# Moving the first pair's token tiles into memory that attention frees first, and loading them at attention's end

## The chip, the cores and the metric

The kernel runs on one core of a Trainium2 chip. The metric is the time of one execution on the device in microseconds (us), taken as the median over several runs. Five engines work side by side, each through its own queue in order: TensorE (PE; its weight loads are shown apart as PEld), VectorE (DVE), ScalarE (ACT), GpSimd (POOL) and SyncE (SP, which here only issues DMA transfers). A DMA that must wait for something holds up whatever stands behind it on the engine that issues it.

## The reference

An attention with mixing of heads before and after the softmax, and a feed-forward part on its result. Cut to what is computed:

```python
# q, k, v: (8, 12, 448, 64); w_pre, w_post: (12, 12)
scores = 1 / sqrt(64) * q @ k^T
scores = einsum('bhij,hg->bgij', scores, w_pre)
attn = exp(scores - max(scores))
attn = attn / (sum(attn) + 1e-9)
attn = einsum('bhij,hg->bgij', attn, w_post)
x = (attn @ v).transpose(0, 2, 1, 3).reshape(3584, 768)
h = x @ w_in            # w_in: (768, 2048)
g = h - tanh(h)
out = g @ w_out         # w_out: (2048, 768)
```

## The kernel before

**Numbers in two parts.** A product of 32-bit numbers is made of three matmuls on rounded parts: each operand is split into a high part (a rounding copy on ScalarE) and a low part (the operand minus its high part, on VectorE); `products` adds high x high, high x low and low x high in one PSUM bank. Names ending in `h` and `l` are such parts. A low part is written over the tile that held the operand.

**Attention** runs as a list of places, `for p in range(NPL + 3)`. At each place it mixes, exponentiates and normalizes one pair of row groups and does jobs planned beforehand (scores, transposes, values). Its results go to DRAM (`xs`, one tensor for each of the 8 batches), through the tile `x` and the DMA queue kept by hand in `dma`, `issue` and `now`. Beside it, until place NPL-3, runs the conversion of the feed-forward weights into parts and sums (`conv`), which go to DRAM too (`wis`, `sss`, `wos`, `tss`).

**The feed-forward part** takes the 3584 tokens in 7 blocks of 512. Block 0 is computed plainly: `Block0.step` runs for f = 0 to 17, where step f loads the weights of f+2 (`load_w0`, three buffers, so the load of f+2 waits until TensorE is through with f-1), calls `between(f)`, multiplies (18 matmuls into one of two PSUM banks `ps_h`), and copies the bank out (L347). Every two steps one gate, h - tanh(h), is computed for two tiles by class `Gate`: `a1` and `a2` on ScalarE (four passes), `d1` and `d2` on VectorE (three), then `a3` on ScalarE (a Relu that serves as a mask), `d3` and `d4` on VectorE (a product and a predicated copy). For small h a rational formula is used, for others tanh; the mask decides. The first two steps of block 0 and its gates run while attention's last values are computed.

The other 6 blocks go in 3 pairs (`pair_step`, 8 steps for each pair), in a scheme with seven products in place of eight. Its right operands are token tiles: `b11`, `b21`, `b22` and `t1` to `t4`, each with parts `h` and `l`, 14 tiles of 3x512 numbers per partition. Four of them (`b11l`, `b21l`, `t3l`, `b22l`) are loaded by `load_xq`, six DMAs each, and `xq_jobs` then makes the 14 tiles from them in eleven jobs: differences on VectorE, high parts on ScalarE (L569), low parts on VectorE (L572). `WA` is the order in which the seven products read them: b11, b21, t2, t1, t3, b22, t4. The products of a step share two banks X and Y of `ps_h`; products 2, 4 and 6 add onto X, which must have been copied out to `h01` or `h23` before. The second gate of a step (`Late`) is computed during the next step; its results and sums of them (`ga`, `gb`, `gs`) are stored by POOL. Between products stand units of the output product (`res.units`), which reads stored gates (`gl<-go`, `gl<-gs`) and weights (`w<-wo`, `w<-ts`). After each pair some units are held back, and the jobs of the next pair's token tiles are run between them.

**Memory.** SBUF is used as two stacks of tile pools, "left" and "right". A pool that is opened over memory of a closed one makes the first user of each tile wait for the last user of what lay there. During attention the left stack holds `ld` (k and q tiles and their parts), `sp` (scores) and `cv` (conversion); it is closed at place NPL-3 and `open_early` opens the first feed-forward pools there. The right stack holds attention's constants, `kp` (`x`, `at`, `vr`) and `gp` (`t`, `e`, `wr`), which are used until attention's end; `open_late` opens pools there after it. In the kernel before, the working tiles of the gates (pool `rw`), the tiles `gl` and `gh` and two weight tiles lie on the left, and all token tiles but one (pool `xqb`) on the right. `close_plain`, at step f=15, closes the pools of block 0's weights and tokens and opens those of the pair's weights (`wa`) there.

**Order.** `in_order`, at the end, fixes the order of every engine's instructions as the program wrote them. So the place in the program where a job stands is its place in the engine's queue.

Of the kernel before, what the change touches and what calls it, by code (L numbers as in the profile page):

```python
# [150 lines left out]
def kernel_body(  # L151
# [71 lines left out]
    def pool(name, bufs, side, stack=ctx):  # L223
        return stack.enter_context(tc.tile_pool(name=name, bufs=bufs, side=side, reuse_waits="tile"))

    def open_early():
        ff.rw = pool("rw", 1, "left")
        ff.bias = pool("bias", 1, "left").tile([P, 2 * LINE], F32, name="bias", tag="bias")
        nc.gpsimd.memset(ff.bias[:, 0:1], GATE_A[1])
        nc.gpsimd.memset(ff.bias[:, 1:2], GATE_B[1])  # L230
        nc.gpsimd.memset(ff.bias[:, 2:3], -0.25)
        ff.gpl, ff.gph, ff.xr = pool("gpl", 3, "left"), pool("gph", 2, "left"), pool("xr", 1, "left")
        ff.w2a, ff.xqa = pool("w2a", 1, "left"), pool("xqa", 1, "left")
        ff.plain = ctx.enter_context(ExitStack())
        ff.w0, ff.xp = pool("w0", 3, "left", ff.plain), pool("xp", NK, "left", ff.plain)

# [7 lines left out]

    def open_late():
        rest_of_line(ctx)
        ff.xqb, ff.ca = pool("xqb", 1, "right"), pool("ca", 3, "right")
        ff.ps_y = ctx.enter_context(tc.tile_pool(name="ps_y", bufs=1, space=PSUM, side="left"))

    def close_plain():  # L250
        ff.plain.close()
        ff.w2b, ff.wap, ff.cb = pool("w2b", 1, "left"), pool("wa", 7, "left"), pool("cb", 9, "left")

    def work(tag, n=2):
        return ff.rw.tile([P, n, TB], F32, name=tag, tag=tag)


    def runs(b):
# [34 lines left out]

    class Gate:

        def __init__(self, h):
            self.h = h

        def a1(self):
            self.u, self.qa = work("u"), work("qa")  # L300
# [13 lines left out]
            nc.vector.scalar_tensor_tensor(out=self.qa, in0=self.qb, scalar=GATE_B[2], in1=self.qa, op0=ALU.add, op1=ALU.mult)  # L314

        def a3(self):
            nc.scalar.activation(self.qb, self.u, AF.Relu, bias=ff.bias[:, 2:3], scale=1.0)

        def d3(self, out):
            nc.vector.tensor_mul(out, self.qa, self.u)  # L320

        def d4(self, out):
            nc.vector.copy_predicated(out, self.qb.bitcast(I32), self.t)


    class Block0:
# [36 lines left out]
    class Results:  # L363
# [38 lines left out]
        def more_w2(self, upto):  # L402
            while self.n_w2 < min(upto + 1, len(self.w2s)):
                x = self.n_w2 % 3
                if self.deep_w2 is not None:
                    x = (self.n_w2 - self.deep_w2) % (len(XQ) + 3) - len(XQ)
                if x < 0:
                    w = ff.xqb.tile([P, HK, TB], F32R, name=XQ[x] + "h", tag=XQ[x] + "h")
                    w = w.rearrange("p c t -> p (c t)").rearrange("p (c t n) -> p c t n", t=2, n=P)
                else:  # L410
                    w = (ff.w2a if x < 2 else ff.w2b).tile([P, NK, 2, P], F32R, name=f"w2{x}", tag=f"w2{x}")
                ff.w2[self.n_w2] = w
                self.w2s[self.n_w2][1](w)
                self.n_w2 += 1

        def more_gr(self, upto):
            while self.n_gr < min(upto + 1, len(self.grs)):
                x = -1
                if self.deep_gr is not None:
                    x = (len(XQ) - 1 - self.n_gr + self.deep_gr) % (len(XQ) + 2) - 3  # L420
                if x < 0:
                    g = ff.gpl.tile([P, 2, TB], F32R, name="gl", tag="gl")
                else:
                    g = ff.xqb.tile([P, HK, TB], F32R, name=XQ[x] + "l", tag=XQ[x] + "l")[:, :2]
                ff.gr[self.n_gr] = g
                self.grs[self.n_gr](raw(g))
                self.n_gr += 1
# [46 lines left out]
        def c_tile(self):  # L474
            x = self.n_c % 12
            self.n_c += 1
            return (ff.ca if x < 3 else ff.cb).tile([P, HK, P], F32, name="c", tag="c")

        def y_tile(self, x):
            return ff.ps_y.tile([TT, TB], F32, name=f"y{x}", tag=f"y{x}")  # L480
# [68 lines left out]

    def x_tiles(*names):  # L550
        for x in names:
            p = ff.xqa if x == "t4l" else ff.xqb
            ff.xs[x] = p.tile([P, HK, TB], F32R, name=x, tag=x)

    def load_xq(name, b, h):
        x_tiles(name)
# [5 lines left out]
    def xq_jobs():  # L562

        def sub(x, y):
            nc.vector.tensor_sub(xr, x if x is xr else raw(ff.xs[x]), y if y is xr else raw(ff.xs[y]))

        def high(x, src):
            x_tiles(x + "h")
            nc.scalar.copy(ff.xs[x + "h"], src)  # L569

        def low(x, src):
            nc.vector.tensor_sub(ff.xs[x + "l"], src, raw(ff.xs[x + "h"]))  # L572

        def both(x):
            high(x, raw(ff.xs[x + "l"]))
            low(x, raw(ff.xs[x + "l"]))

        xr = ff.xr.tile([P, HK, TB], F32, name="xr", tag="xr")
        sub("t3l", "b11l")
        yield  # L580
        both("b11")
        yield
        x_tiles("t1l")
        high("t1", xr)
        low("t1", xr)
        yield
        sub("b22l", xr)
        yield
        x_tiles("t2l")
        high("t2", xr)  # L590
        low("t2", xr)
        yield
        sub("b21l", xr)
        yield
        x_tiles("t4l")
        high("t4", xr)
        low("t4", xr)
        yield
        both("b21")
        yield  # L600
        sub("b22l", "t3l")
        yield
        high("t3", xr)
        low("t3", xr)
# [56 lines left out]
    def pair_step(s, q, late, units, between):  # L661
# [62 lines left out]
    with ExitStack() as st:  # L724
# [508 lines left out]
        for p in range(NPL + 3):  # L1233
# [48 lines left out]
    xq = iter(())  # L1282

    def xq_loads(s):
        ba, bb = 2 * s + 1, 2 * s + 2
        for x, b, h in (("b11l", ba, 0), ("b21l", ba, 1), ("t3l", bb, 0), ("b22l", bb, 1)):
            yield from load_xq(x, b, h)

    xq, xl = xq_jobs(), xq_loads(0)
    res = Results()  # L1290
    ff.n_wa, ff.stored = 0, [0] * NS

    def between0(f):
        if f >= 3:
            for _ in range(4 if f % 2 else 2):
                next(xl, None)
        if f in (10, 12):
            res.more_w2((f - 10) // 2)
        if f in (13, 15):
            res.more_gr((f - 13) // 2)  # L1300
# [13 lines left out]
    for s in range(NS):  # L1314
# [15 lines left out]
        else:  # L1330
            res.deepen()
        job = partial(next, xq, None)
        jobs = [
            [late.v0], [late.v1, late.v2], [late.v3], [late.v4], [late.v5, job], [job, job], [job, job], [job, job],
            [job, job], [job, job],
        ]
        n = HELD[s] + AHEAD[s]
        for i in range(0, n, 2):
# [43 lines left out]
```

## Time and profile before

| | us |
|---|---|
| median of 3 runs (least to greatest) | 1756.36 (1755.81 to 1759.52) |
| profiled execution | 1768.5 |
| its span, first to last instruction | 1766.8 |
| TensorE busy | 1692.2 |
| VectorE busy | 1232.0 |
| ScalarE busy | 1145.3 |
| first matmul of block 0, f=0 (L285) | 868.09 |
| first matmul of the first pair | 945.38 |

The times of the profile are us from the start of the span. A row of the order of time gives start, length, engine, line of the kernel, operation, what is written from what is read, shapes, how many in a row, and in square brackets how long the engine stood idle before it and what released it. A row of waits gives who waited for whom, total us, how often, the longest. A row of groups gives busy us, mean ns of one, then the idle time before. A row of windows gives the busy time of each engine in a stretch, the clock granted to TensorE (1.00 is full), the busy share of the DMA engines and what they moved in GB/s.

### The profile page before, as it was taken

Reading aid. Unit: us, or ns where it says so; the run is one execution under the profiler, and the core shown is the slowest. Engines: PE = TensorE matmul, PEld = TensorE weight load, DVE = VectorE, ACT = ScalarE, POOL = GpSimd, SP = SyncE. Lnnn points to the kernel's source line nnn. Section 1 sums busy time; section 2 is a strip of 40 time slices with the busy share of each in tenths; the row PEclk is TensorE's granted clock in tenths of the full one; section 3 lists DMA queues with packets and bytes.
Section 4 is the critical chain, followed back from the end, with each engine's and each line's share of the span. In section 5 each row is a group of like instructions: output and inputs, shape, how many; then the busy total and the mean of one; then the engine's idle time right before and its main releaser. Section 6 shows DMA issues by size and latency. Waiting matters only on the chain.

```text
span 1766.8 us, 41167 instructions
## 1 busy us (share of the span) xinstructions
PE 1692.2 (96%) x16068; PEld 1399.9 (79%) x16068; DVE 1232.0 (70%) x2119; ACT 1145.3 (65%) x2016; POOL 489.1 (28%) x702
## 2 busy tenths in 40 slices
PE   8999999999999999999997999899999799999999
PEld 6777777777777677777775788788888788989999
DVE  5676777766777767775368899668777767778432
ACT  5776777768878777876476677455666456666331
POOL 1355455555555545451100011011001101001000
PEclk9998999999999989999998999999999999999999
DMA  8778789788887978865497789989889879888994
GB/s 184 201 226 238 226 253 273 223 256 236 246 259 233 263 227 246 258 203 173 166 309 269 243 305 310 318 279 328 324 303 366 320 251 334 300 313 319 405 415 156
DMA packets 322289, 475.09 MB, mean 269 GB/s; under 512 B 105264, under 2 KB 255280, under 8 KB 322096
## 3 DMA queue, kind: packets, MB, share of 16 engines
q1 hardware_dynamic: 305660, 414.34, 73.0%
q0 software_dynamic: 16128, 57.68, 8.3%
q8 instruction: 128, 2.10, 0.5%
q14 instruction: 65, 0.53, 0.1%
q10 hardware_dynamic: 308, 0.43, 0.1%
HBM read 274.73 MB, written 120.59 MB: 224 GB/s over the span
## 4 chain that ended last, share of the span: by engine, by line
PE 77%; DMA 6%; ACT 6%; DVE 6%; issue 3%; SPq 1%; POOL 1%; DVEq 0%; ACTq 0%; POOLq 0%
PE ps_o L945 14%; PE ps_m L987 8%; PE ps_p L906 8%; PE ps_h L285 7%; PE ps_h L286 6%; PE ps_h L288 6%; PE ps_q L862 6%; PE y L527 6%; PE y L525 6%; PE y L526 6%; DMA vr<-in_v_dram 1%; PE ps_m L828 1%; DMA t3l<-xs 1%; ACT e L917 1%; ACT at L955 1%
## 5 line engine op out<-in xcount | busy, mean ns | idle before, releaser
L945 PEld LDWEIGHTS ps_o<-wr,e 60*112 60x112 f32 (+1 forms) x5760 | 308.0, 176 | 46.6 <-POOL wr L928 12.4
L945 PE MATMUL ps_o<-wr,e 60*112 60x60 f32 (+1 forms) x5760 | 317.7, 260 | 17.6 <-ACT at L955 12.3
L915 DVE TENSOR_REDUCE mx<-ps_p 128x1 f32<-128x448 f32 x360 | 207.2, 617 | 165.0 <-PE ps_p L906 164.8
L917 ACT ACTIVATE e<-ps_p,mx 128x448 f32<-128x448 f32 x360 | 225.7, 634 | 106.6 <-DVE mx L915 98.7
L955 ACT COPY at<-ps_o 112x960 f32<-112x960 f32 x156 | 153.7, 985 | 88.3 <-PE ps_o L945 87.6
L928 POOL TENSOR_TENSOR wr<-wpost,zs 128x120 f32<-128x120 f32 x180 | 69.8, 388 | 437.6 <-DVE zs L927 330.1
L906 PE MATMUL ps_p<-t,wpre 60*64 60x448 f32 (+1 forms) x1440 | 186.1, 585 | 4.7 <-DMA t<-s 3.5
L987 PEld LDWEIGHTS ps_m<-at,vr 112*64 112x64 f32 x3072 | 152.2, 140 | 29.2 <-ACT at L962 11.2
L987 PE MATMUL ps_m<-at,vr 112*64 112x120 f32 (+1 forms) x3072 | 166.7, 266 | 5.4 <-ACT at L962 3.1
L525 PE MATMUL y<-w,gh 128*128 128x384 f32 x448 | 153.7, 343 | 5.5 <-DMA w<-ts 3.7
L527 PE MATMUL y<-w,gl 128*128 128x384 f32 x424 | 145.7, 344 | 8.5 <-DVE gl L443 8.4
L526 PE MATMUL y<-w,gh 128*128 128x384 f32 x448 | 152.8, 341 | 0.0
L862 PEld LDWEIGHTS ps_q<-kk,qh 64*120 64x120 f32 (+1 forms) x768 | 62.0, 182 | 88.9 <-issue 61.8
L862 PE MATMUL ps_q<-kk,qh 64*120 64x448 f32 (+1 forms) x768 | 127.3, 408 | 2.2 <-DVE kk L814 1.4
L867 DVE COPY s<-ps_q 120x448 f32<-120x448 f32 (+1 forms) x192 | 112.9, 615 | 11.3 <-PE ps_q L862 11.1
L301 ACT ACTIVATE u<-h 128x1024 f32<-128x1024 f32 x56 | 59.5, 1062 | 67.4 <-DVE h L704 66.5
L867 ACT COPY s<-ps_q 120x448 f32<-120x448 f32 (+1 forms) x192 | 95.5, 539 | 7.0 <-PE ps_q L862 6.7
L657 POOL DMA_DIRECT2D gs<-gb x24 | 17.2, 718 | 297.7 <-DVE gb L656 282.1
L525 PEld LDWEIGHTS y<-w,gh 128*128 128x128 f32 x448 | 86.0, 192 | 11.2 <-ACT u L301 4.0
L437 ACT CAST gh<-gl 128x1024 fp32r<-128x1024 f32 x61 | 63.5, 1040 | 47.6 <-DMA gl<-gs 21.3
L527 PEld LDWEIGHTS y<-w,gl 128*128 128x128 f32 x424 | 81.4, 192 | 10.3 <-DVE gl L443 10.1
L526 PEld LDWEIGHTS y<-w,gh 128*128 128x128 f32 x448 | 85.9, 192 | 3.4
(370 smaller groups left out, 3895.5 us busy)
## 6 DMA issues: line engine op xcount, KB each, us to landing
t<-s SPq DMA_DIRECT2D x342, 210.0 KB
wa<-ss SPq DMA_DIRECT2D x96, 384.0 KB
w<-wo SPq DMA_DIRECT2D x43, 768.0 KB
gl<-gs SPq DMA_DIRECT2D x62, 512.0 KB
wa<-wi SPq DMA_DIRECT2D x72, 384.0 KB
w<-ts SPq DMA_DIRECT2D x35, 768.0 KB
gs<-gs POOLq DMA_DIRECT2D x24, 768.0 KB, 8.9
cr<-in_moe_w_in_dram SPq DMA_DIRECT2D x48, 256.0 KB
```

Source lines behind the costliest of these rows:

```text
L285: nc.tensor.matmul(ph, w[:, c, 0], xh, start=start and c == 0, stop=False, skip_group_check=True)
L525: nc.tensor.matmul(y, gh[:, tok], wh, start=first, stop=False, skip_group_check=True)
L526: nc.tensor.matmul(y, gh[:, tok], wl, start=False, stop=False, skip_group_check=True)
L527: nc.tensor.matmul(y, gl[:, tok], wh, start=False, stop=last, skip_group_check=True)
L862: nc.tensor.matmul(ps[:n, :S], qx[a, hp, :], kx[a, hp % 2], start=(x == 0), stop=(x == 2))
L867: eng(sts[i][:n, 2 * hp + j, :], ps[:n, :S])
L906: nc.tensor.matmul(pss[r][halves[j], :], wpre[k, :], ts[j][k, :], start=True, stop=True)
L915: nc.vector.tensor_reduce(out=mx, in_=ps, axis=AX.X, op=ALU.max, negate=True)
L917: nc.scalar.activation(e, ps, AF.Exp, bias=mx, scale=1.0, accum_out=zs[:, 0, r : r + 1])
L945: nc.tensor.matmul(ps[:CP, j, c * GP : (c + 1) * GP].rearrange("p (h i) -> p h i", i=GI)[:, :, r * GH : (r + 1) * GH], e[k, c * CP : (c + ...
L955: nc.scalar.copy(ats[i0][:, :, :, at : at + 2 * GI].rearrange("p c h (j i) -> p j (c h) i", j=2), ps[:CP, :, : NC * GP].rearrange("p j (x ...
L987: nc.tensor.matmul(pv[j * D : (j + 1) * D, r, :n], vt[:, j, c, :], ats[i][:, c, 2 * hp + j, :n], start=(c == 0), stop=(c == NC - 1),)
```

## The change

Pools are moved: the left stack, from place NPL-3 on, holds the tiles `h01` and `h23` of the gates (pool `hid`), the difference tile `xr` and eleven of the fourteen token tiles (`xqa`). The other gate tiles, `gl`, `gh` and two weight tiles go to the right stack, opened at attention's end, with the three token tiles named in `LATER`. Of the twelve tiles `c` one instead of three lies on the right.

The loads of the first pair's four tiles move from steps f=3 to 8 of block 0 into attention's last places, NPL-2 to NPL+2 (2, 3, 3, 2 and 2 pieces of two DMAs), in the order b11l, t3l, b22l, b21l. The first job on them is issued before step f=1, the others by a list of steps up to f=14. Before, the jobs stood at f=6, 8 and 10 to 15 with three more in the pair's first step. The order of the eleven jobs is changed for all pairs. After the first and second pairs, nine instead of eleven jobs are run among the held units, and two in the next pair's first step.

Step f=2 of block 0, the first with a gate, now stands after `now()` and `open_late()`, not before.

The mask of block 0's gates and of the second gate of each pair step goes to a tile of its own, the one of `gs`, instead of over `qb`; the first gate of a pair step keeps `qb`.

```diff
     def open_early():
-        ff.rw = pool("rw", 1, "left")
+        ff.hid = pool("hid", 1, "left")
...
-        ff.gpl, ff.gph, ff.xr = pool("gpl", 3, "left"), pool("gph", 2, "left"), pool("xr", 1, "left")
-        ff.w2a, ff.xqa = pool("w2a", 1, "left"), pool("xqa", 1, "left")
+        ff.xr, ff.xqa = pool("xr", 1, "left"), pool("xqa", 1, "left")
...
     def open_late():
         rest_of_line(ctx)
-        ff.xqb, ff.ca = pool("xqb", 1, "right"), pool("ca", 3, "right")
+        ff.rw, ff.gpl, ff.gph = pool("rw", 1, "right"), pool("gpl", 3, "right"), pool("gph", 2, "right")
+        ff.w2a, ff.xqb, ff.ca = pool("w2a", 1, "right"), pool("xqb", 1, "right"), pool("ca", 1, "right")
...
-        ff.w2b, ff.wap, ff.cb = pool("w2b", 1, "left"), pool("wa", 7, "left"), pool("cb", 9, "left")
+        ff.w2b, ff.wap, ff.cb = pool("w2b", 1, "left"), pool("wa", 7, "left"), pool("cb", 11, "left")

     def work(tag, n=2):
-        return ff.rw.tile([P, n, TB], F32, name=tag, tag=tag)
+        return (ff.hid if tag in ("h01", "h23") else ff.rw).tile([P, n, TB], F32, name=tag, tag=tag)
+
+    LATER = ("b21h", "b22h", "t4h")
+
+    def x_tile_of(x):
+        return (ff.xqb if x in LATER else ff.xqa).tile([P, HK, TB], F32R, name=x, tag=x)
...
         def a3(self):
-            nc.scalar.activation(self.qb, self.u, AF.Relu, bias=ff.bias[:, 2:3], scale=1.0)
+            self.mk = work("gs", 3)[:, :2] if self.own_mask else self.qb
+            nc.scalar.activation(self.mk, self.u, AF.Relu, bias=ff.bias[:, 2:3], scale=1.0)
...
         def d4(self, out):
-            nc.vector.copy_predicated(out, self.qb.bitcast(I32), self.t)
+            nc.vector.copy_predicated(out, self.mk.bitcast(I32), self.t)
...
         sub("t3l", "b11l")
         yield
+        x_tiles("t1l")
+        parts("t1")
+        yield
+        sub("b22l", "t3l")
+        yield
+        parts("t3")
+        yield
+        nc.vector.tensor_add(xr, xr, raw(ff.xs["b11l"]))
+        yield
         both("b11")
         yield
         x_tiles("t2l")
-        high("t2", xr)
-        low("t2", xr)
+        parts("t2")
         yield
         sub("b21l", xr)
         yield
...
         both("b21")
         yield
...
         both("b22")
         yield
+        x_tiles("t4l")
+        parts("t4")
+        yield
...
-        g1 = Gate(h01)
+        g1 = Gate(h01, False)
...
+        def between0(f):
+            if f in (10, 12):
+                res.more_w2((f - 10) // 2)
+            if f in (13, 15):
+                res.more_gr((f - 13) // 2)
+            for _ in range({1: 2, 2: 1, 4: 1, 5: 1, 6: 1, 8: 1, 10: 1, 12: 1, 14: 1}.get(f, 0)):
+                next(xq)
+
+        xq, xl = xq_jobs(), xq_loads(0)
+        pieces = {NPL - 2: 2, NPL - 1: 3, NPL: 3, NPL + 1: 2, NPL + 2: 2}
...
             for f in start.get(p, ()):
                 f()
-        for _ in range(2):
-            block0.step()
+            for _ in range(pieces.get(p, 0)):
+                next(xl)
+        next(xq)
+        block0.step(between0)
         now()

     open_late()
...
+    block0.step(between0)
...
-    def between0(f):
-        if f >= 3:
-            for _ in range(4 if f % 2 else 2):
-                next(xl, None)
...
-        if 6 <= f < NF and f not in (7, 9):
-            next(xq, None)
...
             [late.v0], [late.v1, late.v2], [late.v3], [late.v4], [late.v5, job], [job, job], [job, job], [job, job],
-            [job, job], [job, job],
+            [job, job],
```

More of the change, by code (lines that the diff above doesn't have):

```diff
@@ L294, in kernel_body, with __init__ @@
     class Gate:
-        def __init__(self, h):
-            self.h = h
+        def __init__(self, h, own_mask=True):
+            self.h, self.own_mask = h, own_mask
         def a1(self):
@@ L407, in more_w2 @@
                 if x < 0:
-                    w = ff.xqb.tile([P, HK, TB], F32R, name=XQ[x] + "h", tag=XQ[x] + "h")
+                    w = x_tile_of(XQ[x] + "h")
                     w = w.rearrange("p c t -> p (c t)").rearrange("p (c t n) -> p c t n", t=2, n=P)
@@ L423, in more_gr @@
                 else:
-                    g = ff.xqb.tile([P, HK, TB], F32R, name=XQ[x] + "l", tag=XQ[x] + "l")[:, :2]
+                    g = x_tile_of(XQ[x] + "l")[:, :2]
                 ff.gr[self.n_gr] = g
@@ L476, in c_tile @@
             self.n_c += 1
-            return (ff.ca if x < 3 else ff.cb).tile([P, HK, P], F32, name="c", tag="c")
+            return (ff.ca if x < 1 else ff.cb).tile([P, HK, P], F32, name="c", tag="c")
         def y_tile(self, x):
@@ L551, in x_tiles @@
         for x in names:
-            p = ff.xqa if x == "t4l" else ff.xqb
-            ff.xs[x] = p.tile([P, HK, TB], F32R, name=x, tag=x)
+            ff.xs[x] = x_tile_of(x)
     def load_xq(name, b, h):
@@ L578, in xq_jobs, with parts @@
         xr = ff.xr.tile([P, HK, TB], F32, name="xr", tag="xr")
+        def parts(x):
+            high(x, xr)
+            low(x, xr)
         sub("t3l", "b11l")
+        yield
[7 more added lines that the diff above has]
+        nc.vector.tensor_add(xr, xr, raw(ff.xs["b11l"]))
         yield
@@ L582, in xq_jobs @@
         yield
[L583 to L588, printed above, removed]
         x_tiles("t2l")
-        high("t2", xr)
-        low("t2", xr)
+        parts("t2")
         yield
@@ L594, in xq_jobs @@
         yield
[L595 to L598, printed above, removed]
         both("b21")
[L600 to L604, printed above, removed]
         yield
@@ L607, in xq_jobs, with xq_loads @@
         yield
+        x_tiles("t4l")
+        parts("t4")
+        yield
     IDLE = ("u", "qa", "qb", "t", "h01", "h23")
+    def xq_loads(s):
+        ba, bb = 2 * s + 1, 2 * s + 2
+        order = (("b11l", ba, 0), ("b21l", ba, 1), ("t3l", bb, 0), ("b22l", bb, 1))
+        for x, b, h in order if s else (order[0], order[2], order[3], order[1]):
+            yield from load_xq(x, b, h)
     WA = (("a11", "b11"), ("a12", "b21"), ("s2", "t2"), ("s1", "t1"), ("s3", "t3"), ("s4", "b22"), ("a22", "t4"))
@@ L1275, in kernel_body @@
                 f()
-        for _ in range(2):
-            block0.step()
+            for _ in range(pieces.get(p, 0)):
+                next(xl)
+        next(xq)
+        block0.step(between0)
         now()
     open_late()
[L1282 to L1289, printed above, removed]
+    block0.step(between0)
     res = Results()
     ff.n_wa, ff.stored = 0, [0] * NS
-    def between0(f):
-        if f >= 3:
-            for _ in range(4 if f % 2 else 2):
-                next(xl, None)
[L1297 to L1300, printed above, removed]
-        if 6 <= f < NF and f not in (7, 9):
-            next(xq, None)
     while block0.f < NF + 2:
@@ L1333, in kernel_body @@
         jobs = [
-            [late.v0], [late.v1, late.v2], [late.v3], [late.v4], [late.v5, job], [job, job], [job, job], [job, job],
-            [job, job], [job, job],
+            [late.v0], [late.v1, late.v2], [late.v3], [late.v4], [late.v5, job], [job, job], [job, job], [job, job], [job, job],
         ]
```

## The prediction

> **What bounds the kernel now.** I read the page, then the windows around the place where attention hands over to the feed-forward part, then TensorE's waits there, then the order of time on TensorE, ScalarE, VectorE and SyncE.
>
> ```profile
> PE 1692.2 (96%) x16068; PEld 1399.9 (79%) x16068; DVE 1232.0 (70%) x2119; ACT 1145.3 (65%) x2016; POOL 489.1 (28%) x702
> ```
>
> ```profile
> 868.00:878.00 10.00, 10.00 (x119) 8.35 (x117) 1.40 (x5) 2.29 (x5) 2.73 (x3) 0.83 0.26 86
> 878.00:897.00 19.00, 19.00 (x85) 15.71 (x85) 6.69 (x7) 9.43 (x11) 0.73 (x1) 1.00 0.63 198
> 897.00:912.00 15.00, 11.29 (x48) 8.45 (x47) 11.06 (x9) 8.94 (x11) 0.54 (x1) 1.00 1.02 364
> 912.00:943.60 31.60, 31.60 (x140) 25.93 (x139) 28.06 (x22) 24.09 (x26) 1.60 (x3) 1.00 0.87 307
> 943.60:971.40 27.80, 18.07 (x63) 12.84 (x62) 23.08 (x18) 20.26 (x21) 1.60 (x3) 0.82 0.68 237
> 971.40:1130.00 158.60, 149.22 (x695) 123.00 (x695) 138.95 (x133) 104.70 (x114) 16.01 (x22) 0.98 0.87 299
> ```
>
> ```profile
> PE ps_h L285 <- ACT h L677: 3.8, 1, 3.8
> PE ps_h L285 <- DMA w<-wi: 3.7, 3, 1.9
> ```
>
> The columns of the windows are length, then busy time (and instructions) of PE, PEld, DVE, ACT, POOL, granted clock, DMA share, GB/s. TensorE is busy 96% of the span, so only the holes count, and the largest lie here. 897 to 912, where the 24 loads of token tiles share the DMA engines (share 1.02) with the weights: 3.7 us idle. 943.6 to 971.4, the end of block 0 and the first products of the first pair: 9.7 us idle, and the clock at 0.82 in the rest. Just before these, 868 to 878 has DMA share 0.26, and 868 to 897 has DVE busy 8.1 of 29 us: the work that is late afterwards could have been done there. From 971 on TensorE is busy 149.2 of 158.6 us, so what is won ahead of that point is kept.
>
> ```profile
> 882.00 0.39 PE L285 MATMUL ps_h<-xh,w 128*128 128x512 f32 x1
> ...
> 886.08 0.39 PE L285 MATMUL ps_h<-xh,w 128*128 128x512 f32 x1
> ...
> 900.41 0.47 PE L285 MATMUL ps_h<-xh,w 128*128 128x512 f32 x1 [1.93 <-DMA w<-wi]
> ...
> 939.62 0.50 PE L285 MATMUL ps_h<-xh,w 128*128 128x512 f32 x1
> ...
> 945.38 0.50 PE L285 MATMUL ps_h<-b11h,wa 128*128 128x512 f32 x1 [1.39 <-ACT h L347]
> ...
> 951.36 0.80 PE L285 MATMUL ps_h<-b21h,wa 128*128 128x512 f32 x1 [3.64 <-ACT h L347]
> ...
> 963.38 0.50 PE L285 MATMUL ps_h<-t2h,wa 128*128 128x512 f32 x1 [3.76 <-ACT h L677]
> ...
> 971.33 0.40 PE L285 MATMUL ps_h<-t3h,wa 128*128 128x512 f32 x1
> ```
>
> Block 0's step f=2 starts at 882.00 and f=3 at 886.08, so a step is 4.08 us; f=15 should start at 882.00+13x4.08=935.04 and starts at 939.62, 4.6 us late: 3.7 us in the three weight waits, the rest in first matmuls after a wait. Then products 0, 1, 2 and 4 of the pair start at 945.38, 951.36, 963.38 and 971.33.
>
> ```profile
> 894.44 0.59 ACT L347 COPY h<-ps_h 128x512 f32<-128x512 f32 x1 [0.59 <-PE ps_h L288]
> ...
> 899.07 0.56 ACT L347 COPY h<-ps_h 128x512 f32<-128x512 f32 x1
> 900.74 1.15 ACT L317 ACTIVATE qb<-u,bias 128x1024 f32<-128x1024 f32 x1 [1.11 <-DVE qa L314]
> ...
> 953.92 1.15 ACT L317 ACTIVATE qb<-u,bias 128x1024 f32<-128x1024 f32 x1 [2.61 <-DVE qa L314]
> ...
> 962.76 0.57 ACT L677 COPY h<-ps_h 128x512 f32<-128x512 f32 x1
> ```
>
> ```profile
> 877.91 0.65 DVE L1005 COPY x<-ps_m 128x210 f32<-128x210 f32 x2 [1.18 <-PE ps_m L987]
> ...
> 897.20 1.23 DVE L310 SCALAR_TENSOR_TENSOR qa<-qa,h 128x1024 f32<-128x1024 f32 x1 [1.84 <-ACT qa L302]
> ...
> 902.06 1.38 DVE L323 COPY_PREDICATED ga<-qb,t 128x1024 f32<-128x1024 int32 x1
> 907.05 1.76 DVE L565 TENSOR_TENSOR xr<-t3l,b11l 128x1536 f32<-128x1536 f32 x1 [3.60 <-DMA t3l<-xs]
> ...
> 965.97 0.68 DVE L683 TENSOR_TENSOR h<-ps_h,h 128x512 f32<-128x512 f32 x1
> ```
>
> Product 2 adds onto bank X, so it waits for ScalarE's copy of X (L677, 962.76). TensorE sits 3.8 us for it. That copy stands behind block 0's last two gates, and these wait for VectorE: the mask's Relu (L317) stands still for d2 (L314) each time, 2.61 us at 953.92. The first token job on VectorE (`t3l` minus `b11l`) starts at 907.05, after waiting for its load, and all eight token jobs of block 0 fall into f=6 to 15: DVE is busy 28.1 of 31.6 us there, and three jobs more spill into the pair.
>
> **The change part by part.**
>
> *Loads.* The token tiles now lie over k, q and score tiles, whose last readers are done by then, so the 24 transfers of the four `l` tiles can move from f=3 to 8 into places NPL-2 to NPL+2. On SyncE they now stand ahead of the weights of f=1, 2 and 3 and of attention's last store.
>
> ```profile
> 843.25 7.96 SPq L895 DMA_DIRECT2D t<-s  x6
> ...
> 855.14 7.24 SPq L268 DMA_DIRECT2D xl<-xs  x12
> ...
> 882.61 0.57 SPq L754 DMA_DIRECT2D xs<-x  x1
> ...
> 896.98 5.28 SPq L559 DMA_DIRECT2D t3l<-xs  x6
> ```
>
> The 12 loads ahead of them take 7.24 us to issue, 0.60 each, up to 862.4, where before only weights followed. By 0.60 the 24 take 14.4 us: SyncE is through by some 878; by the slow row (`t3l`, 5.28 for 6, 0.88 each) 21.1 us, by 885. The weights of f=3 stand last and are due at 886.08; by bytes, 24 transfers of 3.1 MB and three weight tiles of 0.8 MB are 5.5 MB, 15 us at the 364 GB/s of the third window, 23 us at the 237 of the fifth: landed between 878 and 886. The first is nearer, since the window they go into has share 0.26. I take nothing, and keep +0 to +5 us. Gain: the weights of f=6 to 8 lose their competitor, -4.6 us (0 if the weights were late for another reason, which the share of 1.02 speaks against).
>
> *Gates' tiles* (`u`, `qa`, ... in memory that `x`, `at`, `vr` held). First use is the gate of f=0 and 1, after f=2's product, at 886.1. VectorE's last copy into `x` ends at 878.6 (877.91 plus 0.65), and the store that reads `x` goes out after f=1's step instead of at 882.61, behind the token loads: from 878.6 on. How long such a store takes is not shown; the nearest is the sums' store of the first pair:
>
> ```profile
> DMA to landing us min/median/max: 6.1/8.1/11.1
> ```
>
> With its 6.1 to 11.1 us the store has landed between 884.7 and 889.7, and the gate is 0 to 3 us late; with its 8.1 it lands at 886.7, when the gate's first pass starts. I take 0 (0 to 3). TensorE would not wait for this gate, only the lag below would grow.
>
> *Token jobs.* The same eleven, 1.75 us each on VectorE, seven with a 1.47 us high part on ScalarE (two adds of one form become others: no change in count). They start after the copy at 877.91 instead of at 907.05, five by f=4 and the rest one each at f=5, 6, 8, 10, 12, 14; none is left for the pair.
>
> ```profile
> L569 ACT CAST t1h<-xr 128x1536 fp32r<-128x1536 f32 x1 | 1.5, 1469 | 0.0
> ```
>
> ```profile
> L572 DVE TENSOR_TENSOR t1l<-xr,t1h 128x1536 fp32r<-128x1536 f32 x1 | 1.8, 1774 | 0.0
> ```
>
> A gate takes VectorE 902.06+1.38-897.20=6.2 us per two steps, with a job 8.0, against 8.16 for two steps of TensorE: it keeps up. ScalarE: 894.44 to 899.63 is 5.2, Relu 1.15, high part 1.47, 7.8 us: it keeps up too. The pair of steps 4 and 5 has two jobs (9.7) and starts a lag of some 2 us, which falls by 0.2 to 0.3 per two steps to some 1 us at the end.
>
> *Mask.* a3 writes its own tile, so ScalarE no longer waits for d2 (1.1 to 2.8 us each in block 0); for g1 of a pair it stays.
>
> Walk at the end of block 0: f=15 ends at 935.04+4.08=939.1. VectorE, lagging 1 us, begins gate 6 (steps 12, 13) at 939 and ends it at 945.1; then the first `gl` until 946.3. ScalarE: copy of f=15 until 940.7, Relu 941.7, `gh` 942.7, gate 7's four passes as VectorE frees `u` and `t` (943.8, 945.1) until 947.9, Relu 949.0, then L677. VectorE ends gate 7 at 952.4, then L683, 953.1. TensorE: product 0 from 939.9, product 1 from 943.0 (its weights need f=15 done), unit until 948, product 2 at 949.6 (before: 963.38), product 3 at 953.1 after L683 (before L683 started at 965.97), unit, product 4 at 957.2 instead of 971.33: -14.1 us with the 4.6 in it. Bounds: without lag L683 ends near 951, -16; with 5 us of lag near 957, -10.
>
> *Clock.* The walk has holes of 1.1 to 1.6 us. What a hole costs:
>
> ```profile
> 1399.52 0.44 PE L527 MATMUL y<-w,gl 128*128 128x384 f32 x1 [2.68 <-DVE gl L443]
> 1399.80 0.33 PE L525 MATMUL y<-w,gh 128*128 128x384 f32 x1
> ...
> 1401.39 0.53 PE L527 MATMUL y<-w,gl 128*128 128x384 f32 x1
> ```
>
> After 1.39 and 1.93 us (945.38, 900.41) the next matmul takes 0.50 and 0.47 and the stretch runs on at full clock; after 2.68 us (1399.52) the matmul that takes 0.33 next takes 0.53 at 1401.39, after 3.64 us (951.36) it takes 0.80. Mine lie below, nearest to 1.39; but they come in a row, so I take +1 us (0 to 3). The Trainium skill, TensorE: Matmul & The Clock Gate, Part 1: The HAM clock gate, says that the clock is halved after an idle window of about 3.4 us; by it the holes cost nothing and the sum would be 1 us better, but the row after 2.68 us shows a shorter hole paying.
>
> *Later pairs.* Two jobs slip from the tail of the second pair into the next pair's first step, where no gate runs, and VectorE no longer waits for the ScalarE part of the same iteration.
>
> ```profile
> 1413.58 0.44 PE L527 MATMUL y<-w,gl 128*128 128x384 f32 x1 [3.52 <-DVE gl L443]
> ```
>
> Of this 3.52 us I walk out 1.3 gained (0 to 3).
>
> Sum: -14.1+1-1.3=-14.4. Profiled execution 1768.5 us, so 1754.1; the median shown is 1756.36, 12 us lower than the profiled one, so 1742.0.
>
> **The rivals.**
>
> Crowding: the token loads hold up the weights of f=3 and TensorE with them. For it: 0.88 us per issue, and loads that SyncE issued beside weights went slowly. Against: DMA share 0.26. At the slow end of both sums above the weights come some 5 us late: 1747.
>
> Gates stay the bound: the lag at steps 4 and 5 doesn't fall, product 4 comes at 963. Gain 8: 1748.
>
> More than forecast: no lag, no throttled stretch and all of 3 us in the later pairs, -16-3=-19: 1737.
>
> Nothing moves: the token tiles wait for memory that is freed late, loads start where they did. Against it: the last gathers out of the score tiles are issued by 851. 1754 to 1757.
>
> Slower: the mask now stands in the tile of the sums, so the Relu of a pair waits for the store of the step before.
>
> ```profile
> 1034.74 0.75 POOL L658 DMA_DIRECT2D gs<-gs  x1
> ```
>
> ```profile
> 1045.45 0.60 ACT L692 ACTIVATE h<-ps_h 128x512 f32<-128x512 f32 x1 [0.50 <-DVE t L311]
> ```
>
> Issued at 1034.74, wanted at 1045.45+0.60, 11.3 us later; landing takes 8.1 us, at most 11.1. It decides once landing exceeds 11.3 by 2 us in the seven such steps of the first pair (there VectorE is busy 139 of 158.6 us and goes to TensorE's accumulators right after): above 13.3 us. At 15 us: 7x3.7=26 lost less 14 gained, 1768.
>
> **How the numbers follow.** Forecast 0.66 (1738 to 1747); crowding 0.09; gates as bound 0.08; more 0.07; nothing moves 0.05; slower 0.05. Of these 1735 to 1750 leaves out the last two and the ends where two mishaps add up (crowding with lag, 1752), some 2 in 10. A measurement of this kernel tells no less than about 0.2%, 3.5 us, from no change: the first four cases are faster by more (0.90), nothing moves is within it (0.05), the last is slower (0.05).
>
> **What would show it.** The steps are right if there is no TensorE wait for `w<-wi` between f=5 and f=8; if `t3l` minus `b11l` runs on VectorE before 881; if f=15 starts 53 us after f=2 and product 4 of the first pair some 75 us after f=2 (before 89.3); and if L317 waits for VectorE only in the first gate of a pair's step. They are wrong with a wait for `w<-wi` at f=2 or 3, the first gate's L301 waiting for a DMA, L317 waiting for a DMA in the first pair, DVE over 9 tenths from f=6 on.

## The result and the profile after

The changed kernel takes 1743.08 us (median of 4 executions, 1740.96 to 1746.34), the kernel before 1756.09 us (4, 1754.44 to 1759.52): a ratio of 0.9925, 95% interval 0.9902 to 0.9948. The profiled execution took 1741.7 us, its span 1740.0.

The two profiled spans differ by 26.8 us, but that isn't the change. Block 0's step f=2 starts at 882.00 us before and at 869.81 after, and the 12.2 us between them lie in attention. There the same code varies: in the profiles told of here f=2 starts between 870.0 and 882.0 in the four kernels with the old memory (mean 874.8) and between 869.8 and 878.6 in the eight with the new one (mean 873.7). So readings that compare kernels count from the start of f=2. From there to the end it was 884.8 us before and is 870.2 after, **14.6 us less**; the forecast sum was 14.4.

The windows of the changed kernel, same columns as before:

```profile
856.00:875.00 19.00, 19.00 (x155) 15.75 (x155) 6.81 (x8) 5.21 (x8) 1.30 (x3) 0.90 0.87 278
875.00:890.00 15.00, 15.00 (x68) 12.41 (x67) 13.02 (x10) 13.39 (x16) 0.73 (x1) 1.00 0.74 245
890.00:922.00 32.00, 32.00 (x143) 26.51 (x142) 31.38 (x26) 29.04 (x32) 2.13 (x4) 1.00 0.86 293
922.00:946.00 24.00, 19.42 (x87) 14.87 (x86) 19.65 (x17) 16.24 (x18) 1.60 (x3) 1.00 0.93 338
946.00:1110.00 164.00, 156.18 (x738) 129.53 (x737) 139.66 (x134) 105.16 (x116) 17.45 (x24) 0.99 0.86 298
```

The loads' crowd (DMA share 1.02 at 897 to 912 before, 3.7 us of TensorE idle) is gone: 890 to 922 has share 0.86 and no hole. The stretch at the end of attention is filled instead, 0.87 where 0.26 stood. At the handover, 922 to 946, TensorE is idle 4.6 us, where 9.7 stood before. Its waits between 868 and 972:

```profile
PE ps_h L290 <- ACT h L688: 1.3, 1, 1.3
PE ps_h L290 <- DVE h L694: 1.1, 1, 1.1
PE ps_h L290 <- ACT gh L443: 1.0, 1, 1.0
PE y L503 <- DVE gl L449: 0.9, 1, 0.9
PE ps_h L290 <- DVE h L715: 0.7, 1, 0.7
PE ps_h L290 <- DMA wa<-wi: 0.3, 1, 0.3
```

No `w<-wi` is among them. (Lines have shifted: L285, L317, L347, L677 and L683 are L290, L323, L353, L688 and L694 now.) TensorE's matmuls in order of time, the start of f=2, of f=15 and of products 0, 1, 2, 3 and 4:

```profile
869.81 0.39 PE L290 MATMUL ps_h<-xh,w 128*128 128x512 f32 x1
```

```profile
922.85 0.39 PE L290 MATMUL ps_h<-xh,w 128*128 128x512 f32 x1
...
927.35 0.47 PE L290 MATMUL ps_h<-b11h,wa 128*128 128x512 f32 x1 [0.26 <-DMA wa<-wi]
...
930.61 0.47 PE L290 MATMUL ps_h<-b21h,wa 128*128 128x512 f32 x1 [0.97 <-ACT gh L443]
...
937.51 0.50 PE L290 MATMUL ps_h<-t2h,wa 128*128 128x512 f32 x1 [1.33 <-ACT h L688]
...
940.99 0.50 PE L290 MATMUL ps_h<-t1h,wa 128*128 128x512 f32 x1 [1.12 <-DVE h L694]
...
945.25 0.40 PE L290 MATMUL ps_h<-t3h,wa 128*128 128x512 f32 x1
```

Counted from f=2, f=15 starts at 53.04 us (before 57.62), product 2 at 67.70 (81.38), product 3 at 71.18 (84.83) and product 4 at 75.44 (89.33): 13.9 us earlier at the place where the walk said 14.1. VectorE and SyncE in order of time:

```profile
866.19 1.76 DVE L570 TENSOR_TENSOR xr<-t3l,b11l 128x1536 f32<-128x1536 f32 x1
...
877.28 1.23 DVE L315 SCALAR_TENSOR_TENSOR qa<-qa,h 128x1024 f32<-128x1024 f32 x1 [0.93 <-ACT qa L307]
...
895.64 1.24 DVE L315 SCALAR_TENSOR_TENSOR qa<-qa,h 128x1024 f32<-128x1024 f32 x1
...
926.88 1.21 DVE L315 SCALAR_TENSOR_TENSOR qa<-qa,h 128x1024 f32<-128x1024 f32 x1
```

```profile
848.66 1.85 SPq L564 DMA_DIRECT2D b11l<-xs  x4
...
865.54 0.32 SPq L283 DMA_DIRECT2D w<-wi  x1
866.39 0.57 SPq L765 DMA_DIRECT2D xs<-x  x1
```

The first token job runs at 866.19, 3.6 us ahead of f=2 (before: 25.05 us behind it). The columns of SyncE's rows are those of its queue: 24 loads issued from 848.66 to 865.33, the last early weight right behind, the store of `x` at 866.39.

One execution of the kernel e6 below took 3823 us at the full clock; the ratio given for that kernel leaves it out.

### The profile page after: what moved, and what is told of

Read it like the earlier page. It is cut to its first block, busy times and chain, and to the rows that moved or that the text cites. A ratio compares the mean times of both kernels' runs of the same rounds, so it can differ in the third digit from the quotient of the medians.

```text
span 1740.0 us, 41171 instructions
## 1 busy us (share of the span) xinstructions
PE 1673.0 (96%) x16068; PEld 1391.5 (80%) x16068; DVE 1232.8 (71%) x2119; ACT 1142.9 (66%) x2016; POOL 489.3 (28%) x702
## 4 chain that ended last, share of the span: by engine, by line
PE 76%; DVE 8%; DMA 6%; ACT 6%; issue 3%; SPq 1%; POOL 1%; DVEq 0%; ACTq 0%; POOLq 0%
PE ps_o L956 14%; PE ps_m L998 8%; PE ps_p L917 8%; PE y L533 6%; PE y L531 6%; PE y L532 6%; PE ps_h L290 6%; PE ps_h L291 6%; PE ps_h L293 6%; PE ps_q L873 6%; DMA vr<-in_v_dram 1%; PE ps_m L839 1%; DVE qa L319 1%; DMA t<-s 1%; DMA gl<-gs 1%
## 5 line engine op out<-in xcount | busy, mean ns | idle before, releaser
L956 PEld LDWEIGHTS ps_o<-wr,e 60*112 60x112 f32 (+1 forms) x5760 | 306.1, 175 | 45.2 <-POOL wr L939 12.2
L917 PE MATMUL ps_p<-t,wpre 60*64 60x448 f32 (+1 forms) x1440 | 180.9, 570 | 7.0 <-DMA t<-s 5.1
L998 PEld LDWEIGHTS ps_m<-at,vr 112*64 112x64 f32 x3072 | 147.5, 137 | 29.5 <-ACT at L973 11.5
L998 PE MATMUL ps_m<-at,vr 112*64 112x120 f32 (+1 forms) x3072 | 161.8, 261 | 6.8 <-ACT at L973 4.1
L443 ACT CAST gh<-gl 128x1024 fp32r<-128x1024 f32 x61 | 63.4, 1039 | 52.6 <-DMA gl<-gs 17.4
```

The costliest lines, as they stand in the source:

```text
L917: nc.tensor.matmul(pss[r][halves[j], :], wpre[k, :], ts[j][k, :], start=True, stop=True)
L956: nc.tensor.matmul(ps[:CP, j, c * GP : (c + 1) * GP].rearrange("p (h i) -> p h i", i=GI)[:, :, r * GH : (r + 1) * GH], e[k, c * CP : (c + ...
L998: nc.tensor.matmul(pv[j * D : (j + 1) * D, r, :n], vt[:, j, c, :], ats[i][:, c, 2 * hp + j, :n], start=(c == 0), stop=(c == NC - 1),)
```

## The experiments

This table is worked out from the starts in order of time on TensorE, in us after the start of f=2, each kernel's profiled execution; the last column but one is the span's end. The parts of the change are priced at product 4, which starts at 75.44, 75.47 and 75.47 us in the three profiles with the same first pair (after, a0, e5); the ratios can't price them, since the intervals of after, a0, e1 and e2 overlap. Ratios are to the kernel before on the same chip, with 95% intervals.

| kernel | f=15 | product 2 | product 4 | end | ratio |
|---|---|---|---|---|---|
| before | 57.62 | 81.38 | 89.33 | 884.8 | |
| after | 53.04 | 67.70 | 75.44 | 870.2 | 0.9925 [0.9902, 0.9948] |
| a0, after | 53.04 | 67.73 | 75.47 | 869.6 | 0.9946 [0.9922, 0.9971] |
| e1, after, mask over `qb` | 54.43 | 73.65 | 81.43 | 873.2 | 0.9954 [0.9929, 0.9979] |
| e2, after, jobs late | 53.74 | 72.06 | 82.86 | 873.5 | 0.9958 [0.9938, 0.9977] |
| e3, after, loads and jobs late | 57.35 | 75.67 | 86.64 | 878.7 | 0.9993 [0.9971, 1.0015] |
| e4, before, mask moved | 56.41 | 74.65 | 85.65 | 879.9 | one execution |
| e8, before, loads by POOL | 57.59 | 81.35 | 89.35 | 882.0 | 1.0008 [0.9985, 1.0031] |
| e11, before, both | 55.11 | 75.56 | 86.53 | 878.9 | one execution |
| e5, after, old order later | 53.04 | 67.74 | 75.47 | 869.6 | 0.9928 [0.9902, 0.9954] |
| e6, after, last gate in the pair | 53.04 | 66.23 | 72.44 | 863.7 | 0.9910 [0.9878, 0.9943] |
| e10, e6, later loads by POOL | 53.04 | 66.25 | 72.43 | 856.8 | 0.9876 [0.9845, 0.9907] |

In e2, e3, e4, e8, e11 and before, token jobs stand in the pair's first step too.

a0 is the changed kernel once more, on the chip of e5, e6 and e10, to compare them with:

> The changed kernel once more, beside the variants of this group. Product 4 of the first pair at 75 to 76 us after the start of block 0's step f=2, the stretch from product 4 to the end within 3 us of the kernel before, time 10 to 16 us below the kernel before.

Product 4 came as expected, the stretch behind it is 1.4 us shorter than before, and the time is 9.3 us below the kernel before (1747.59 and 1756.84), just short of the 10 to 16.

The first theory was the prediction's: the weights' waits, the late jobs and the Relu's wait each have a price, and these add up. The rival: they are bounds side by side, and taking one away alone shows little, because the next stands just behind it.

**e1: the mask back over `qb`.**

```diff
-        def __init__(self, h, own_mask=True):
+        def __init__(self, h, own_mask=False):
```

> The changed kernel, with the mask written over qb again in every gate; loads and token jobs stay early. Counted from the start of block 0's step f=2, the changed kernel starts product 4 of the first pair (tile t3h) at 75.4 us. Theory (the early token jobs carry the transition, the mask is a minor term): ScalarE waits for d2 again, 1.1 us or more in each of block 0's eight gates, high parts come that much later, product 4 at 76 to 79, time 1744 to 1748. Rival (the mask is what frees ScalarE): product 4 at 84 or later, time 1751 or more.

ScalarE's waits and then TensorE's, of e1, around the handover:

```profile
ACT qb L323 <- DVE qa L319: 11.3, 8, 2.5
```

```profile
PE ps_h L290 <- ACT h L688: 3.7, 1, 3.7
```

Product 4 comes at 81.43, 6.0 us later than after, between the theory's 76 to 79 and the rival's 84. With the jobs early, ScalarE still stands 11.3 us for d2, and the copy of X (L688) is late by it. The mask, to which the prediction gave no price of its own, carries 6.0 of the 13.9 us in the finished kernel.

That is a price at product 4. At the end 3.0 of the 6.0 are left (873.2 and 870.2 in the table). The first product of the third pair's last step still starts 4.8 us later than after (703.0 and 698.2 us behind f=2); from there on the 928 matmuls take 170.2 us in e1 and 172.0 in after, at a granted clock of 1.00 and 0.99.

**e2: the loads early, the jobs where they stood.**

```diff
-            for _ in range({1: 2, 2: 1, 4: 1, 5: 1, 6: 1, 8: 1, 10: 1, 12: 1, 14: 1}.get(f, 0)):
-                next(xq)
+            if 6 <= f < NF and f not in (7, 9):
+                next(xq, None)
...
-        xq, xl = xq_jobs(), xq_loads(0)
+        xq, xl = xq_jobs(True), xq_loads(0)
...
-        next(xq)
```

Here `xq_jobs(True)` is the old order of the eleven jobs.

> The changed kernel, with the first pair's eleven token jobs at the old steps (f=6, 8, 10 to 15 and three in the pair) and in the old order; the loads stay at attention's end. Theory (two separate gains, weights in time 4.6 us and jobs out of the way 9.4 us): no wait for w<-wi in block 0, f=15 at 53 us after f=2, product 4 at 81 to 85, time 1749 to 1753. Rival (the early loads alone carry the gain): product 4 at 75 to 77, time 1742 to 1745.

TensorE's waits of e2:

```profile
PE ps_h L290 <- DVE h L722: 2.8, 1, 2.8
PE ps_h L290 <- ACT h L353: 2.5, 1, 2.5
...
PE ps_h L290 <- DMA w<-wi: 0.4, 1, 0.4
```

Product 4 at 82.86: the early jobs are worth 7.4 us at product 4 once the loads are early and the mask is free; at the end 3.3 of them are left. Their wait moves to the accumulations on VectorE (2.8) and the bank's copy (2.5). The 0.4 us for a weight, at f=3, is the only crowding by the early loads that any of these kernels showed.

**e3: memory and mask alone.** e2, and the loads back where they stood. In the program that is f=3 to 6, as the expectation says, and not f=3 to 8, as is said further up.

```diff
+            if f >= 3:
+                for _ in range(4 if f % 2 else 2):
+                    next(xl, None)
...
-            for _ in range(pieces.get(p, 0)):
-                next(xl)
```

> The changed kernel's memory, mask and later pairs, but the first pair's loads back at f=3 to 6 of block 0 and its jobs at the old steps in the old order. Theory: the waits for w<-wi in block 0 are back (3 to 5 us), f=15 at 57 to 58 us after f=2, product 4 at 86 to 89 (89.3 in the kernel before), time 1752 to 1756. Rival (where the tiles lie is what counts, not when they are loaded): product 4 below 80, time below 1747.

TensorE's waits of e3:

```profile
PE ps_h L290 <- DMA w<-wi: 2.4, 1, 2.4
```

Product 4 at 86.64, as expected, with a weight late again by 2.4 us, less than the 3 to 5 expected. With old jobs and a free mask the early loads are worth 86.64-82.86=3.8 us; new memory and mask together 89.33-86.64=2.7. The ratio can't be told from 1.

**e8: the kernel before, its 24 first-pair loads issued by POOL.** This takes them out of SyncE's queue and leaves their place in the program.

```diff
-                nc.sync.dma_start(raw(ff.xs[name])[:, c, to], xs[i][:, h * HK + c, at])
+                (nc.gpsimd if b < 3 else nc.sync).dma_start(raw(ff.xs[name])[:, c, to], xs[i][:, h * HK + c, at])
```

> The kernel before, with only the 24 loads of the first pair's token tiles issued by POOL instead of SyncE, at the same steps. It tells why the weights of f=6 to 8 came late. If SyncE's queue was blocked by the token loads: no wait for w<-wi, f=15 at 53 to 54 us after f=2 (57.6 before), and the time 2 to 4 us below the kernel before. If the DMA engines were full (share 1.02): the waits for w<-wi stay at 3 to 5 us and the time stays.

The waits of e8 between f=2 and the first pair, TensorE, ScalarE, VectorE:

```profile
PE ps_h L285 <- ACT h L347: 8.0, 7, 3.6
```

```profile
ACT qb L317 <- DVE qa L314: 18.2, 8, 5.1
```

```profile
DVE xr L565 <- DMA t3l<-xs: 4.2, 1, 4.2
```

No wait for `w<-wi` is left, and steps f=6 to 9 start at 16.32, 20.40, 24.48 and 28.56, on time to 0.01 us. From 15 to 30 us after f=2 (885.04 to 900.04) the DMA engines move 364 GB/s at share 1.00, as they did before at 897 to 912 (364 at 1.02), and TensorE is busy 15.00 of 15.00 us. So the weights had been late for their place behind the token loads in SyncE's queue, and the full DMA engines by themselves did not make them late. Yet, against the expectation of 53 to 54 and of a gain, f=15 starts at 57.59 (57.62 before) and product 4 at 89.35 (89.33). TensorE now waits 8.0 us in seven places for ScalarE's copy of a bank, ScalarE 18.2 us for d2 (15.4 before), VectorE 4.2 us for `t3l` (3.6 before), so that the first token job starts 0.6 us later (25.66). The 4.6 us of the weights, taken away with no more than this beside it, are worth nothing: the lag of ScalarE and VectorE stood right behind them.

**e4: the kernel before with the mask moved. e11: e4 and e8 together.**

```diff
+            self.mk = work("gs", 3)[:, :2] if self.own_mask else self.qb
-            nc.scalar.activation(self.qb, self.u, AF.Relu, bias=ff.bias[:, 2:3], scale=1.0)
+            nc.scalar.activation(self.mk, self.u, AF.Relu, bias=ff.bias[:, 2:3], scale=1.0)
...
-        g1 = Gate(h01)
+        g1 = Gate(h01, False)
```

> The kernel before with only the mask moved to a tile of its own (block 0's gates and second gates); memory, loads and jobs as before. If the place of the tiles in memory costs and wins nothing by itself: as the variant with the new memory and the mask and the old loads and jobs, f=15 at 57 to 58 us after f=2, product 4 at 86.6 (86 to 87.5), and waits for w<-wi of 2 to 4 us. If the new memory took part in that variant's 2.7 us: product 4 nearer to 89.3.

> The same, with the first pair's 24 loads issued by POOL. Without the mask this took the weight waits away and moved product 4 by 0.0. If it was the Relu's wait for VectorE that took their place (TensorE waited 8.0 us for L347): with the mask in a tile of its own the weights now pay, f=15 at 53 to 54, product 4 at 82 to 84, as with early loads and late jobs (82.9). If something else took their place: product 4 stays at 86 to 87.

VectorE's wait for its loads, of e4 and of e11:

```profile
DVE xr L566 <- DMA b22l<-xs: 1.3, 1, 1.3
```

```profile
DVE xr L566 <- DMA b22l<-xs: 5.1, 1, 5.1
```

The mask alone moves product 4 by 3.7 us, to 85.65, a little more than expected (86 to 87.5); f=15 comes at 56.41 (57 to 58). With the new memory (e3) product 4 is 1.0 us later than that, so the place of the tiles by itself won nothing. With the weights' competitor gone as well (e11) it comes at 86.53, 0.9 later than in e4 and in the range of "something else took their place". VectorE's wait for its loads grew from 1.3 to 5.1 us, and the first job starts at 26.54 in place of 22.73. From first job to product 4 it is 62.9 us in e4 and 60.0 in e11; if product 4 hangs on the first job, the weights gave some 2.9 us and the later loads took more. This split is worked out, not run by itself.

**e5: the later pairs in the old order**, all eleven jobs among the held units.

```diff
-            xq = xq_jobs()
+            xq = xq_jobs(True)
...
-            [job, job],
+            [job, job], [job, job],
```

> The changed kernel, with the token jobs of the second and third pair in the old order and all eleven among the held units. Theory of the prediction: the later pairs lose 1 to 2 us to it, product 4 of the first pair unchanged at 75.4. Rival: the new order gives in one place (VectorE's low parts before the third pair) what it takes in another (ScalarE's copies of the results in the first pair's tail, a wait of 1.4 us that the kernel before doesn't have), and the time stays within 1 us.

From product 4 to the end it is 794.1 us in e5, 794.1 in a0, 794.8 in after and 795.5 before. The waits for `gl` (L449) from 975 on are 8.8 us in e5 and 6.9 in a0, but a0 has a wait of 1.4 for L509 that e5 lacks, and more at L290; all groups of waits listed from there on sum to 23.5 us and 23.7. By place: between the second and third pair, from the one's last step to the other's first, TensorE is idle 13.2 us in e5 and 11.5 in a0, between the first and second 5.4 and 6.7. That is the rival: what the new order gives in one place it takes in another, and it is worth nothing that can be told.

**e6: block 0's last gate computed in the pair's first step**, as the second gates of pair steps are, so that the copies of banks no longer stand behind it.

```diff
+    class LateBlock0:
+        def __init__(self, g):
+            self.g = g
+            self.v0, self.v1, self.v2 = g.a1, g.a2, g.d1
+        def v3(self):
+            self.out = work("ga")
+            self.g.d2()
+            self.g.a3()
+            self.g.d3(self.out)
+        def v4(self):
+            self.g.d4(self.out)
+            nc.gpsimd.dma_start(gos[:, NF - 2 : NF], self.out)
+        def v5(self):
+            pass
...
-    while block0.f < NF + 2:
+    while block0.f < NF:
...
-    late, left = None, 4 * NQ
+    late, left = LateBlock0(block0.old), 4 * NQ
```

> The changed kernel, with block 0's last gate computed inside the first pair's first step, in the places where the later steps compute the gate held over, instead of ahead of the pair. Theory (what is left at the handover is ScalarE's copies of X and Y standing behind that gate): the waits of 1.3 us for L688 and 1.1 us for L694 go, product 4 at 72 to 74 us after f=2 instead of 75.4, time 1 to 3 us below the changed kernel. Rival (the gate is owed anyway, VectorE has no slack in the first pair): what is won at product 2 is lost again by product 6, and the time stays.

TensorE's waits of e6 at the handover:

```profile
PE ps_h L290 <- DMA wa<-wi: 1.4, 1, 1.4
```

The two waits that led the list of after (L688, L694) are gone; the longest is one for a weight of the pair. Product 4 comes at 72.44, 3.0 us earlier than in a0, and the end at 863.7, 5.9 earlier; the two ratios' intervals overlap, so it is the profile that carries this. That there was a wait left at the copy of X was right. Of the further 2.9 us behind product 4, 2.6 lie between the second pair's last step and the third pair's first: 82.3 us in a0 and 79.7 in e6, with TensorE idle 11.5 and 11.6 of them and the granted clock 0.92 and 0.96. So most of the rest is the clock, and no run ties that to this edit.

**e10: e6, with the 48 loads of the later pairs' token tiles issued by POOL.**

```diff
-                nc.sync.dma_start(raw(ff.xs[name])[:, c, to], xs[i][:, h * HK + c, at])
+                (nc.sync if b < 3 else nc.gpsimd).dma_start(raw(ff.xs[name])[:, c, to], xs[i][:, h * HK + c, at])
```

> As the variant with the last gate inside the pair, and the 48 token loads of the second and third pair issued by POOL instead of SyncE. If SyncE's queue is what makes the weights late at the end of the first and second pair (TensorE waits 5.3 us for w<-wo and 1.0 for w<-ts in the changed kernel): these waits go, 3 to 6 us below the variant without this edit. If the DMA engines are full there: the waits stay and the time too.

TensorE's waits from 975 us on, of e6 and then of e10:

```profile
PE y L533 <- DVE gl L449: 7.7, 4, 3.2
PE y L501 <- DMA w<-wo: 5.5, 1, 5.5
PE y L531 <- DMA w<-ts: 3.7, 2, 2.8
```

```profile
PE y L533 <- DVE gl L449: 5.2, 4, 2.2
PE y L501 <- DMA w<-wo: 2.6, 1, 2.6
...
PE y L531 <- DMA w<-wo: 2.0, 2, 1.4
PE y L531 <- DMA w<-ts: 1.8, 1, 1.8
```

The window 1080 to 1100, where the second pair's tokens are loaded, of e6 and of e10; then the last token loads in SyncE's queue and the row that issues the next weights, of e6, and that row of e10:

```profile
1080.00:1100.00 20.00, 14.52 (x74) 12.47 (x73) 15.73 (x14) 11.31 (x12) 2.08 (x3) 0.92 1.03 406
```

```profile
1080.00:1100.00 20.00, 17.37 (x96) 14.91 (x96) 18.86 (x19) 12.69 (x13) 9.75 (x18) 1.00 1.03 394
```

```profile
1084.76 4.29 SPq L564 DMA_DIRECT2D b22l<-xs  x4
...
1089.59 1.22 SPq L375 DMA_DIRECT2D w<-wo  x2
```

```profile
1085.19 4.14 SPq L375 DMA_DIRECT2D w<-wo  x2
```

The waits sum to 22.4 us in e6 and 17.4 in e10, and the end moves by 6.9 us (the two ratios' intervals overlap). The waits for weights (`w`) shrank from 9.2 us to 6.4 and did not go, as was expected; those for `gl`, whose loads (`gl<-go`) SyncE issues too, went from 7.7 to 5.2. The DMA engines are as full as before (share 1.03, 406 and 394 GB/s), so no bandwidth was won; counted from f=2 the weights were issued 5.9 us earlier (218.45 and 212.55), since they no longer stood behind 4.29 us of token loads in SyncE's queue, and TensorE's busy time in the window went from 14.52 to 17.37 us, part of it by the clock (0.92 and 1.00). The Trainium skill, DMA: Bandwidth & Descriptors, Issuing engines are not separate DMA queues, says that transfers started by several engines still share the same 16 engines, and that only time on the issuing sequencer is saved. The share and the GB/s agree. The same section of the Trainium skill calls this time usually small beside the transfer itself. For one load that holds here (`b22l`: 0.43 us to issue in the median of e6, 7.2 us to land in e10), but the four that stood ahead of the weights add up to 4.29 us. How much of the 6.9 us is this order of issue, and how much the order in which the transfers shared the engines, stays open. e10 is the fastest of the kernels here, 1734.89 us against 1756.84 for the kernel before on the same chip, ratio 0.9876, interval 0.9845 to 0.9907.

## Why the prediction was right, step by step

**The walk** held: f=15 at 53.04 (walk 53.04), product 2 at 67.70 (67.6), product 3 at 71.18 (71.1), product 4 at 75.44 (75.2). VectorE's first passes of gates 0, 2 and 6 (877.28, 895.64, 926.88) show the lag: gate 2 is 2.0 us behind two times 8.16, gate 6 only 0.6 behind six times 8.16. That is the 2 us that fall to some 1. One sign named for being wrong did appear, VectorE over 9 tenths from f=6 on: it is busy 31.38 of 32.00 us from 890 to 922. But the walk itself gave it 8.0 of 8.16 us per two steps, so that sign could not tell right from wrong. The first job ran right behind the last copy into `x`, 3.6 us ahead of f=2, as walked.

**The loads.** By the fast row, 0.60 us per issue, SyncE should be through at 878, 4 us ahead of f=2, and the store of `x` should go out 3.4 us ahead; the last early weight was issued 4.3 us ahead, the store 3.4. Crowding, the first rival, did not occur. But "-4.6 us" as the gain of the weights by themselves was the wrong term: e8 took it away alone and won 0.0. The lag of ScalarE and VectorE stood behind it and gave f=15 at the same 57.6. Nor was it the DMA share of 1.02 by itself that made the weights late, as the prediction read it, but their place in SyncE's queue (e8). In company the weights do pay at f=15: 4.6 us with all parts, 3.9 without the early jobs (e2), 3.2 without the mask (e1). The walk, which follows all queues, had the right sum, the list of prices did not.

**The mask.** The step that named it, "ScalarE no longer waits for d2", had the mechanism and no price. It is 6.0 us with the rest in place (e1), 3.7 alone (e4).

**The gates' tiles** cost nothing: ScalarE's first pass of gate 0 starts at 874.94 directly behind its copy, with no wait for a DMA.

**The clock** was put at +1 us for four holes in a row. They came, 0.26, 0.97, 1.33 and 1.12 us ahead of products 0 to 3 and 0.90 in the unit, and the granted clock of 922 to 946 is 1.00: the term is 0. That is what the Trainium skill, TensorE: Matmul & The Clock Gate, Part 1: The HAM clock gate, would have given, with its idle window of about 3.4 us. Shorter holes can pay, though, as the prediction's row had it. TensorE in order of time, later in the changed kernel:

```profile
1371.48 0.52 PE L533 MATMUL y<-w,gl 128*128 128x384 f32 x1 [2.79 <-DVE gl L449]
...
1374.68 0.52 PE L531 MATMUL y<-w,gh 128*128 128x384 f32 x1
...
1375.24 0.33 PE L533 MATMUL y<-w,gl 128*128 128x384 f32 x1
1375.41 0.33 PE L531 MATMUL y<-w,gh 128*128 128x384 f32 x1
```

After 2.79 us idle, matmuls of this form follow each other every 0.32 us until 1375.00, and then every 0.17. So 3.5 us ran at about half speed, some 1.6 us lost. But the length of a hole does not decide this by itself. The same order of time in the changed kernel and then in e5:

```profile
1349.06 0.69 PE L533 MATMUL y<-w,gl 128*128 128x384 f32 x1 [1.91 <-DVE gl L449]
1349.54 0.52 PE L531 MATMUL y<-w,gh 128*128 128x384 f32 x1
```

```profile
936.23 0.47 PE L290 MATMUL ps_h<-b21h,wa 128*128 128x512 f32 x1 [2.81 <-DMA wa<-wi]
936.54 0.39 PE L291 MATMUL ps_h<-b21l,wa 128*128 128x512 f32 x1
```

After 1.91 us the changed kernel runs at half speed (0.52), after 2.81 us e5 runs at full speed (0.39). A hole of 1.87 us at 1626.44 in the changed kernel is followed by 5 us at a granted clock of 0.66, one of 1.91 at the same place in the kernel before (1654.81) by 5 us at 1.00. In the twelve profiles told of here, every hole of 3.0 us or more behind f=2 was followed by a slowed stretch and no hole of up to 1.7 us was, unless a longer one stood close by; between these lengths it went both ways. What decides there is not shown. The holes of the handover, 1.33 us at most, lie below all that.

**The later pairs** were to give 1.3 us and gave none (e5). The step named was right: the wait of 3.52 is 1.89 at the same place (1.87 in a0, 3.51 in e5). What it left out is that waits appear elsewhere, one of 1.46 shortly ahead of it and one of 1.4 for L509 in the first pair's tail. The two misses, +1 and -1.3, cancel, and that is luck: 13.9 us at product 4 and 0.7 behind it make the 14.6.

**The slower rival** would have needed the sums' store to land later than 13.3 us. The store's group and then the Relu's, of the changed kernel:

```profile
DMA to landing us min/median/max: 6.2/9.3/12.0
```

```profile
  DVE qa L319: 12.5, 13
```

It lands after 9.3 us, at most 12.0, and the Relu never waited for a DMA. Its only waits are for VectorE, 12.5 us in 13 places, in the first gates, which keep `qb`; before there were 35.8 us in 36.

**The median.** The prediction took 14.4 us off a profiled execution and then the 12 us by which the median before lay below its profile. That the median difference is 13.0 (9 to 17 by the interval) and the count from f=2 gives 14.6 are one result within what such a measurement tells.

## What to carry to other kernels

Where several engines lag together at a handover, price the parts by walking every queue in order, not by adding up waits: each bound hides the next, so a part taken away alone can show 0.0 us (e8) and 3.8 in company (the loads, from e3 to e2). A temporary that shares a tile makes an in-order engine wait for a reader, and everything queued behind it is late too; look at what stands behind such an instruction, not at its own wait. Ahead of a full DMA stretch, check which transfer is wanted first and what stands ahead of it in the issuing queue.

## What was not expected of the hardware

The attention stage ends up to 12 us apart in profiles of the same attention code (f=2 from 870.0 in e8 to 882.0 before), while from f=2 on three profiles with the same first pair agree within 0.6 us (870.2, 869.6, 869.6: after, a0, e5); the granted clock goes with it, 0.94, 0.97, 0.98 and 0.97 up to 200, 400, 600 and 860 us before against 0.97, 1.00, 0.98 and 0.98 in e8, while TensorE was idle no longer before (30.7 and 33.5 us). Why the clock differs is open, and a profile's span can't be compared with another's without a common start. And issuing a group of loads from POOL can cost or gain by place alone: 24 loads moved in block 0 changed product 4 by 0.0 us and the time by a factor of 1.0008, while 48 moved in the later pairs brought the end 6.9 us forward at an unchanged DMA share where they are loaded.
